# A list-scheduled order for a hash attention with a feed-forward layer: later loads on the Pool queue, more transposes by DMA

## The chip, the cores and the metric

The kernel runs on one core of one Trainium2 chip. The metric is device microseconds (us) of one execution, as the median of several runs. "Span" is the time from the first to the last instruction in the trace; the measured time of this kernel lies about 2 us above it. A run is called slow if it is over 1.5 % above the fastest run of the same kernel; ratios use fast runs alone.

## The reference

```
q, k, v: (4 batches, 8 heads, 768 rows, 64)    proj: (64, 6)
q_bits = (q @ proj > 0);  k_bits = (k @ proj > 0)          # 6 bits, one bucket per row
mask   = bucket(q)[:, None] == bucket(k)[None, :]
attn   = softmax(where(mask, q @ k.T / 8, -1e9)) @ v
x      = attn as (3072 tokens, 512)
h      = max(x @ w1, x @ w2, x @ w3)                        # 512 -> 768
out    = h @ w_out                                         # 768 -> 512, float32
```

A wrong hash bit changes whole rows, so the kernel computes the bits from both an fp16 high part and an fp16 remainder.

## The kernel before

The work comes in 16 pairs of heads (4 batches of 4 pairs). For each pair, q and k are loaded as float32 (`raw`), split into an fp16 high part and an fp16 remainder that lie side by side (`S16`, 128 columns), and transposed to operands (`T`, 128 partitions). Six hash bits per row are computed from all 128 partitions and then written over the first six remainder rows, so that a score is one product of depth 70: the 64 real columns and six columns of plus or minus a large number. Where all six bits agree, the exp's bias brings the score back to size; elsewhere it underflows to zero.

Batches 0 and 1 are transposed by TensorE (PE), batches 2 and 3 by transposing DMAs. All loads of q, k and v and all transposing DMAs go through the SP queue, in a hand-made order of steps.

```
    def load(n, b, pr, eng, heads=(0, 2)):
        h0, h1 = heads
        r_ = raw_tile(n, b, pr)
        src = {"q": q, "k": k, "v": v}[n][b, 2 * pr + h0 : 2 * pr + h1]
        eng.dma_start(r_[:, h0:h1, :], src.rearrange("h (p c) d -> p h (c d)", c=NCH))
    # ... cut ...
    def xbar(n, b, pr):
        nc.sync.dma_start_transpose(T[n, b, pr][:], S16[n, b, pr][:].rearrange("p a d -> p (a d)"))
    # ... cut ...
    def score(u):                                    # two matmuls, then the exp
        # ... cut ...
        nc.scalar.activation(AT[:], sc[:, :, 0:HQ], ActFn.Exp, bias=bias_t[:], scale=EXP_SCALE)
    # ... cut: attend (AT times v, 12 small matmuls per two units), norm, x_T ...
    def push_ffn(b, hf, xT):
        # l1: 4 matmuls of 128x384 into "ps", 18 times; l2: 6 matmuls of 128x512 into "po", 3 times
    # ... cut ...
    for b in range(1, B):
        for pr in range(NP):
            s = 33 + 7 * pr if b == 1 else 2 * (b - 1) * NUG + 4 + 11 * pr
            at(s - 8, lambda b=b, pr=pr: load_pair(b, pr, nc.sync))
            (front if b == 1 else prep)(b, pr, s)        # front: PE transposes; prep: DMA transposes
```

There are 192 score units of two matmuls each, 192 exps, and 8 blocks of the feed-forward layer (FFN; "ps" is its first layer, "po" its second). A block can start only when all four pairs of its half batch have been attended. PE takes its instructions in the order in which they were written: if the next one waits for an operand, all later ones wait too.

The softmax here doesn't subtract the row's maximum and nothing guards it: scores larger than these inputs give would overflow.

Of the kernel before, what the change touches and what calls it, by code (L numbers as in the profile page):

```python
# [8 lines left out]
FP32 = mybir.dt.float32  # L10
# [3 lines left out]


@with_exitstack
def kernel(
# [24 lines left out]
    KR = D + NBITS  # L42

# [5 lines left out]

    konst = ctx.enter_context(tc.tile_pool(name="konst", bufs=1))  # L50
    raw = ctx.enter_context(tc.tile_pool(name="raw", bufs=4))
    spl = ctx.enter_context(tc.tile_pool(name="spl", bufs=3))
    opnd = ctx.enter_context(tc.tile_pool(name="opnd", bufs=8))
    vpool = ctx.enter_context(tc.tile_pool(name="vpool", bufs=2))
    atp = ctx.enter_context(tc.tile_pool(name="atp", bufs=4))
    small = ctx.enter_context(tc.tile_pool(name="small", bufs=4))
    xp = ctx.enter_context(tc.tile_pool(name="xp", bufs=3))
    hp = ctx.enter_context(tc.tile_pool(name="hp", bufs=12))
    op = ctx.enter_context(tc.tile_pool(name="op", bufs=4))
# [5 lines left out]


    raws = {}

    def raw_tile(n, b, pr):
        if (n, b, pr) not in raws:  # L70
            raws[n, b, pr] = raw.tile([P, 2, NCH * D], FP32, tag=n + "32", name=n + "32")
        return raws[n, b, pr]

    def load(n, b, pr, eng, heads=(0, 2)):
        h0, h1 = heads
        r_ = raw_tile(n, b, pr)
        src = {"q": q, "k": k, "v": v}[n][b, 2 * pr + h0 : 2 * pr + h1]
        eng.dma_start(r_[:, h0:h1, :], src.rearrange("h (p c) d -> p h (c d)", c=NCH))
# [3 lines left out]
    load("q", 0, 0, nc.sync, (0, 1))  # L82
    load("k", 0, 0, nc.sync, (0, 1))
    load("q", 0, 0, nc.sync, (1, 2))
    load("k", 0, 0, nc.sync, (1, 2))
    load("v", 0, 0, nc.sync)
    for n in "qkv":
        load(n, 0, 1, nc.sync)

    bias_t = konst.tile([P, 1], FP32, name="bias_t")  # L90
    nc.vector.memset(bias_t[:], EXP_BIAS)
    warm = konst.tile([P, 1], FP32, name="warm")
    nc.scalar.activation(warm[:], bias_t[:], ActFn.Exp)
    iden = konst.tile([P, P], FP16, name="iden")
    make_identity(nc, iden[:])
    ones = konst.tile([P, P], FP16, name="ones")
    nc.vector.memset(ones[:], 1.0)
    vones = []
    for i in range(2):
        t = konst.tile([P, H, NCH, D + 2], FP16, name=f"vone{i}", tag=f"vone{i}")  # L100
        nc.vector.memset(t[:, :, :, D : D + 1], 1.0)
        vones.append(t)

    ph = konst.tile([D, NBITS], FP16, name="ph")
    pr32 = konst.tile([D, NBITS], FP32, name="pr32")
    PA, PB = [], []
    for i in range(2):
        for n, l in (("PA", PA), ("PB", PB)):
            l.append(konst.tile([P, 32], FP16, name=f"{n}{i}", tag=f"{n}{i}"))
            nc.vector.memset(l[i][:], 0.0)  # L110

    def make_p(i):

        if i == 0:
            nc.vector.tensor_copy(ph[:], p32[:])
            nc.vector.tensor_tensor(out=pr32[:], in0=p32[:], in1=ph[:], op=AluOp.subtract)
        for o in (0, D):
            for l, src in ((PA, ph), (PB, pr32)):
                nc.vector.tensor_scalar(out=l[i][o : o + D, NBITS * i : NBITS * (i + 1)], in0=src[:],
                                        scalar1=1024.0, scalar2=None, op0=AluOp.mult)  # L120

    w_sb = [konst.tile([P, NJ, DF], FP16, name=f"w{i}_sb") for i in range(3)]
    wout_sb = konst.tile([P, NF, DM], FP16, name="wout_sb")

    def load_w(i, half):
        w_ap = (moe_w1, moe_w2, moe_w3)[i].rearrange("(c p) f -> p c f", p=P)
        f = slice(half * DF // 2, (half + 1) * DF // 2)
        nc.gpsimd.dma_start(w_sb[i][:, :, f], w_ap[:, :, f])


    T = {}
    S16 = {}

    def operands(b, pr):
        for n in "qk":
            S16[n, b, pr] = spl.tile([P, 2 * NCH, 2 * D], FP16, tag=n + "s", name=n + "s")
            T[n, b, pr] = opnd.tile([P, 2 * NCH, P], FP16, tag=n + "T", name=n + "T")

    def split_h(n, b, pr, eng, heads=(0, 2)):
        a = slice(heads[0] * NCH, heads[1] * NCH)  # L140
        x32 = raws[n, b, pr][:].rearrange("p h (c d) -> p (h c) d", d=D)[:, a, :]
        o = S16[n, b, pr][:, a, 0:D]
        if eng is nc.scalar:
            nc.scalar.activation(o, x32, ActFn.Copy, scale=QS)
        else:
            eng.tensor_scalar(out=o, in0=x32, scalar1=QS, scalar2=None, op0=AluOp.mult)  # L146

    def split_r(n, b, pr, heads=(0, 2)):
        a = slice(heads[0] * NCH, heads[1] * NCH)
        x32 = raws[n, b, pr][:].rearrange("p h (c d) -> p (h c) d", d=D)[:, a, :]  # L150
        s = S16[n, b, pr]
        nc.vector.scalar_tensor_tensor(out=s[:, a, D : 2 * D], in0=x32, scalar=QS,  # L152
                                       in1=s[:, a, 0:D], op0=AluOp.mult, op1=AluOp.subtract)

    def xbar(n, b, pr):
        nc.sync.dma_start_transpose(T[n, b, pr][:], S16[n, b, pr][:].rearrange("p a d -> p (a d)"))

    def pe_T(n, b, pr, hh):
        ps = mm_ps.tile([P, 512], FP32, tag="mm", name="tps")
        p16 = ps[:].bitcast(FP16)  # L160
        for c in range(NCH):
            nc.tensor.transpose(p16[:, c * P : (c + 1) * P], S16[n, b, pr][:, hh * NCH + c, :], iden[:])  # L162
        return p16

    def evac_T(p16, n, b, pr, hh, eng, c0=0, c1=NCH):
        o = T[n, b, pr][:, hh * NCH + c0 : hh * NCH + c1, :].rearrange("p a t -> p (a t)")
        if eng is nc.scalar:
            nc.scalar.copy(o, p16[:, c0 * P : c1 * P])
        else:
            nc.vector.tensor_copy(o, p16[:, c0 * P : c1 * P])  # L170

    def hash_mm(sets):

        hps = mm_ps.tile([P, 512], FP32, tag="mm", name="hps")
        ws = [(i, l[i]) for l in (PA, PB) for i in range(len(sets))]
        for m, (i, w) in enumerate(ws):
            for g, (t, hh, half) in enumerate(sets[i]):
                a = hh * NCH + half * CH
                nc.tensor.matmul(hps[32 * g : 32 * (g + 1), 0:HQ], w[:], t[:, a : a + CH, :],  # L179
                                 start=m == 0, stop=m == len(ws) - 1)  # L180
        return hps

    def hash_cmp(out, hps):
        nc.vector.tensor_scalar(out=out, in0=hps[:, 0:HQ], scalar1=0.0, scalar2=0.5,  # L184
                                op0=AluOp.is_gt, op1=AluOp.subtract)

    def hash_row(dst, src):
        nc.vector.tensor_scalar(out=dst, in0=src, scalar1=2 * BIT, scalar2=None, op0=AluOp.mult)  # L188

    hbs = {}  # L190

    def hash_pair(b, pr):
        hb = small.tile([P, HQ], FP16, tag="hb", name="hb")
        hbs[b, pr] = hb
        g = [(T[n, b, pr], hh) for hh in range(2) for n in "qk"]
        hash_cmp(hb[:], hash_mm([[(t, hh, half) for t, hh in g] for half in range(2)]))
        hash_row(hb[:], hb[:])

    def hash_half(b, pr, half):
        if half == 0:  # L200
            hbs[b, pr] = small.tile([P, S], FP16, tag="hb2", name="hb2")
        g = [(T[n, b, pr], hh, half) for hh in range(2) for n in "qk"]
        hash_cmp(hbs[b, pr][:, half * HQ : (half + 1) * HQ], hash_mm([g]))

    def hash_head_rows(b, pr, hh):
        for i, n in enumerate("qk"):
            dst = T[n, b, pr][D : D + NBITS, hh * NCH : (hh + 1) * NCH, :].rearrange("p a t -> p (a t)")
            o = 32 * (2 * hh + i)
            hash_row(dst, hbs[b, pr][o : o + NBITS, :])

    def hash_rows(b, pr):
        hb = hbs.pop((b, pr))
        for g, (n, hh) in enumerate((("q", 0), ("k", 0), ("q", 1), ("k", 1))):
            for half in range(2):
                a = hh * NCH + half * CH
                o = 32 * g + NBITS * half
                nc.sync.dma_start(T[n, b, pr][D : D + NBITS, a : a + CH, :].rearrange("p a t -> p (a t)"),
                                  hb[o : o + NBITS, :])

    def hash_head(b, pr, hh):  # L220

        tq, tk = T["q", b, pr], T["k", b, pr]
        hb = small.tile([P, HQ], FP16, tag="hb", name="hb")
        hash_cmp(hb[:], hash_mm([[(tk, hh, 0), (tq, hh, 0), (tk, hh, 1), (tq, hh, 1)]]))
        for g, (t, half) in enumerate(((tk, 0), (tq, 0), (tk, 1), (tq, 1))):
            a = hh * NCH + half * CH
            hash_row(t[D : D + NBITS, a : a + CH, :].rearrange("p a t -> p (a t)"),
                     hb[32 * g : 32 * g + NBITS, :])
# [290 lines left out]
```

## Time and profile before

| | before |
|---|---|
| time, median of 3 runs | 308.07 us (307.59 to 308.14) |
| span, mean clock granted to TensorE | 306.0 us, 0.974 |
| PE busy | 276.1 us (90 %) |
| first "ps" matmul | 63.9 us |
| last exp | 281.0 us |

The profile's page: busy time by engine with its share of the span; then the span in 40 equal slices (7.65 us each), a digit being tenths of the slice; then one group of instructions with its busy time and the mean ns of one.

```profile
span 306.0 us, 7090 instructions
...
PE 276.1 (90%) x2896; PEld 176.6 (58%) x2896; DVE 212.0 (69%) x455; ACT 200.6 (66%) x265; POOL 9.3 (3%) x17
...
PE   3847888989969989999999989999999999999994
...
PEclk9969979999997999999999999999999999999998
DMA  7999940006326285915809490926002001100202
...
L269 ACT ACTIVATE AT<-sc,bias_t 128x768 f16<-128x768 f32 x192 | 169.1, 902 | 73.2 <-PE sc L265 72.7
...
```

PE is at nine tenths or more in most slices once the first 60 us are over; the exp takes 902 ns.

The table of stretches of the same kernel: the stretch, its length, busy us and instruction count of each engine, then the granted clock, the mean busy share of the 16 DMA engines and the GB/s moved. The DMA share adds up the recorded times of packets, and it exceeds 1 in places.

```profile
core 0: us, PE busy (x) PEld busy (x) DVE busy (x) ACT busy (x) POOL busy (x), PEclk, DMA share, GB/s
60.00:160.00 100.00, 93.18 (x1044) 60.23 (x1043) 77.83 (x165) 71.01 (x93) 0.00 (x0) 0.98 0.46 121
160.00:280.00 120.00, 118.94 (x1207) 74.83 (x1205) 76.39 (x161) 89.30 (x121) 0.00 (x0) 1.00 0.35 83
...
```

The tile view of the first FFN layer shows the shortest, median and longest matmul in ns and the first and last start:

```profile
...
L329 PE MATMUL ps<-xT,w_sb x576: 322/326/527, 63.9 to 297.3; 128*128 128x384 f16 x192
...
```

The view of waits (us in total, times, longest) shows that ACT waits for scores, that is, for PE, and the longest wait of PE's matmuls for an operand, 4.3 us for a split at the start:

```profile
engine line waited for: us in total, times, longest us
ACT AT L269 <- PE sc L265: 72.7, 101, 5.5
...
PE tps L162 <- DVE qs L152: 11.9, 7, 4.3
...
```

### The profile page before, as it was taken

Reading aid. Unit: us, or ns where it says so; the run is one execution under the profiler, and the core shown is the slowest. Engines: PE = TensorE matmul, PEld = TensorE weight load, DVE = VectorE, ACT = ScalarE, POOL = GpSimd, SP = SyncE. Lnnn points to the kernel's source line nnn. Section 1 sums busy time; section 2 is a strip of 40 time slices with the busy share of each in tenths; the row PEclk is TensorE's granted clock in tenths of the full one; section 3 lists DMA queues with packets and bytes.
Section 4 is the critical chain, followed back from the end, with each engine's and each line's share of the span. In section 5 each row is a group of like instructions: output and inputs, shape, how many; then the busy total and the mean of one; then the engine's idle time right before and its main releaser. Section 6 shows DMA issues by size and latency. Waiting matters only on the chain.

```text
span 306.0 us, 7090 instructions
## 1 busy us (share of the span) xinstructions
PE 276.1 (90%) x2896; PEld 176.6 (58%) x2896; DVE 212.0 (69%) x455; ACT 200.6 (66%) x265; POOL 9.3 (3%) x17
## 2 busy tenths in 40 slices
PE   3847888989969989999999989999999999999994
PEld 1444565656646656565666556656666665666551
DVE  5687996877995867969587677969664454455551
ACT  3425658968646667777778676868676787786220
POOL 1370000000000000000000000000000000000000
PEclk9969979999997999999999999999999999999998
DMA  7999940006326285915809490926002001100202
GB/s 216 372 287 264 227 131 2 3 5 185 132 56 172 45 233 130 222 39 113 249 15 230 114 246 20 237 95 136 2 1 105 2 0 54 53 1 2 103 0 104
DMA packets 46080, 35.20 MB, mean 115 GB/s; under 512 B 26656, under 2 KB 42976, under 8 KB 46048
## 3 DMA queue, kind: packets, MB, share of 16 engines
q1 hardware_dynamic: 42016, 31.61, 37.7%
q0 software_dynamic: 3952, 3.15, 6.5%
q8 instruction: 22, 0.36, 0.5%
q14 instruction: 10, 0.08, 0.1%
q10 hardware_dynamic: 80, 0.00, 0.0%
HBM read 25.17 MB, written 6.29 MB: 103 GB/s over the span
## 4 chain that ended last, share of the span: by engine, by line
PE 74%; DVE 18%; ACT 3%; issue 2%; DMA 1%; SPq 0%; DVEq 0%; ACTq 0%
PE ps L329 28%; PE sc L265 16%; PE av L285 9%; PE po L341 9%; PE hps L179 4%; PE tps L162 4%; DVE qs L152 3%; ACT AT L269 2%; DVE hb L184 2%; DVE ks L146 2%; DVE ks L152 2%; PE xps L315 2%; DVE kT L188 2%; PE svp L244 1%; DVE t L301 1%
## 5 line engine op out<-in xcount | busy, mean ns | idle before, releaser
L269 ACT ACTIVATE AT<-sc,bias_t 128x768 f16<-128x768 f32 x192 | 169.1, 902 | 73.2 <-PE sc L265 72.7
L329 PE MATMUL ps<-xT,w_sb 128*128 128x384 f16 x576 | 112.4, 327 | 1.9 <-DVE ht L336 1.7
L265 PE MATMUL sc<-qT,kT 70*128 70x384 f16 x384 | 96.4, 332 | 4.2 <-ACT AT L269 1.6
L285 PEld LDWEIGHTS <-AT 128*128 128x128 f16 x1152 | 61.3, 98 | 31.1 <-issue 6.9
L336 DVE TENSOR_TENSOR ht<-ht,ps 128x384 f16<-128x384 f16 x96 | 52.9, 552 | 34.4 <-PE ps L329 31.6
L285 PE MATMUL av<-vone,AT 128*128 128x65 f16 x1152 | 67.1, 193 | 4.4 <-DVE t L301 4.3
L329 PEld LDWEIGHTS <-w_sb 128*128 128x128 f16 x576 | 50.8, 98 | 30.9 <-issue 5.8
L265 PEld LDWEIGHTS <-kT 70*128 70x128 f16 x384 | 34.0, 100 | 23.9 <-issue 6.4
L341 PE MATMUL po<-wout_sb,ht 128*128 128x512 f16 x144 | 34.8, 379 | 0.0
L334 ACT CAST ht<-ps 128x384 f16<-128x384 f32 x48 | 22.8, 474 | 16.3 <-PE ps L329 16.1
L301 DVE TENSOR_TENSOR t<-av,mv 128x390 f32<-128x390 f32 x32 | 17.9, 560 | 10.1 <-PE av L285 10.0
L184 DVE TENSOR_SCALAR hb<-hps 128x384 f16<-128x384 f32 x28 | 15.2, 553 | 8.7 <-PE hps L179 8.6
L162 PE MATMUL tps<-iden,qs 128*128 128x128 f16 x96 | 9.7, 259 | 12.7 <-DVE qs L152 11.9
L341 PEld LDWEIGHTS <-ht 128*128 128x128 f16 x144 | 12.8, 97 | 13.1 <-issue 0.6
L347 DVE COPY osb<-po 128x512 f32<-128x512 f32 x16 | 11.0, 688 | 11.5 <-PE po L341 11.5
L305 DVE TENSOR_TENSOR xn<-t,rr 128x384 f16<-128x384 f32 x32 | 17.9, 558 | 1.1
L152 DVE SCALAR_TENSOR_TENSOR qs<-q,qs 128x768 f16<-128x768 f32 (+1 forms) x17 | 16.5, 972 | 0.1
L162 PEld LDWEIGHTS <-qs 128*128 128x128 f16 x96 | 7.4, 116 | 14.7 <-DVE qs L152 13.3
L316 DVE COPY xT<-xps 128x384 f16<-128x384 f16 x32 | 11.3, 353 | 6.2 <-PE xps L315 5.9
L152 DVE SCALAR_TENSOR_TENSOR ks<-k,ks 128x768 f16<-128x768 f32 (+1 forms) x17 | 15.3, 906 | 0.3
L179 PE MATMUL hps<-kT,PA 128*32 128x384 f16 x64 | 11.1, 343 | 1.0 <-DVE kT L170 0.9
L170 DVE COPY kT<-tps 128x768 f16<-128x768 f16 x16 | 8.6, 553 | 4.3 <-PE tps L162 4.2
(43 smaller groups left out, 172.9 us busy)
## 6 DMA issues: line engine op xcount, KB each, us to landing
v<-in_v_dram SPq DMA_DIRECT2D x16, 384.0 KB
out_dram<-osb SPq DMA_DIRECT2D x24, 256.0 KB
q<-in_q_dram SPq DMA_DIRECT2D x15, 384.0 KB
k<-in_k_dram SPq DMA_DIRECT2D x15, 384.0 KB
w_sb<-in_moe_w_dram POOLq DMA_DIRECT2D x6, 384.0 KB, 13.3
wout_sb<-in_moe_w_out_dram POOLq DMA_DIRECT2D x1, 768.0 KB, 22.0
q<-in_q_dram SPq DMA_DIRECT2D x2, 192.0 KB
k<-in_k_dram SPq DMA_DIRECT2D x2, 192.0 KB
```

The source lines that it names most:

```text
L152: nc.vector.scalar_tensor_tensor(out=s[:, a, D : 2 * D], in0=x32, scalar=QS, in1=s[:, a, 0:D], op0=AluOp.mult, op1=AluOp.subtract)
L162: nc.tensor.transpose(p16[:, c * P : (c + 1) * P], S16[n, b, pr][:, hh * NCH + c, :], iden[:])
L179: nc.tensor.matmul(hps[32 * g : 32 * (g + 1), 0:HQ], w[:], t[:, a : a + CH, :], start=m == 0, stop=m == len(ws) - 1)
L184: nc.vector.tensor_scalar(out=out, in0=hps[:, 0:HQ], scalar1=0.0, scalar2=0.5, op0=AluOp.is_gt, op1=AluOp.subtract)
L265: nc.tensor.matmul(sc[:, i, 0:HQ], kT[0:KR, hh * NCH + 2 * j + i, :], qT[0:KR, hh * NCH + hf * CH : hh * NCH + (hf + 1) * CH, :], start=Tr ...
L269: nc.scalar.activation(AT[:], sc[:, :, 0:HQ], ActFn.Exp, bias=bias_t[:], scale=EXP_SCALE)
L285: nc.tensor.matmul(av[:, o : o + D + 1], AT[:, i, c * P : (c + 1) * P], vones[b % 2][:, 2 * pr + hh, 2 * j + i, 0 : D + 1], start=first, s ...
L301: nc.vector.tensor_tensor(out=t[:, :, :, 0 : D + 1], in0=av[:, :, :, 0 : D + 1], in1=mvs[b, pr][:].unsqueeze(2).to_broadcast([P, 2, CH, D ...
L329: nc.tensor.matmul(ps[:, 0:HQ], w_sb[i][:, jc, fb * P : (fb + 1) * P], xT[:, jc, :], start=jc == 0, stop=jc == NJ - 1)
L334: nc.scalar.copy(ht[:], ps[:, 0:HQ])
L336: nc.vector.tensor_tensor(out=hts[fb][:], in0=hts[fb][:], in1=ps[:, 0:HQ], op=AluOp.max)
L341: nc.tensor.matmul(ps[:], hts[fb][:, c * P : (c + 1) * P], wout_sb[:, fb, :], start=fb == 0, stop=fb == NF - 1)
```

## The change

The intent: replace the hand-made steps by a list scheduler that, with planned durations and buffer counts, decides the order of every engine's instructions before the kernel is built; let ready FFN work fill PE where scores are not ready; keep transposes on SP from waiting behind loads (in the kernel before, SP's loads, L78, waited twice for DVE's splits to free a buffer, 17.1 us in all, by the view of SP's waits), by giving the loads of batches 1 to 3 to the Pool queue; score pair 0 one head at a time, as the kernel before already does, so that the first exp needs only one head's operands; take the exp's bias as a constant; compute the hash with T as weights and 12 columns, transpose the bits, and bring them to T through a small DRAM tile. Batch 1's operands and most of x's blocks are now transposed by DMA too: 24 operand transposes where there were 16, each 393 KB as before, and 20 of x where there were none.

The planner's DMA model is worth reading: a transfer takes its planned time, 1.8 times that if another queue is moving data, plus 2 us to land. A transposing DMA of one operand is planned at 2.1 us and a load at 1.1 us.

```diff
+class Plan:
+    LAT = {"PE": 0.22, "DVE": 0.1, "ACT": 0.1, "POOL": 0.1, "SP": 2.0}
... cut ...
+                    if t.xfer:
+                        at = max(dma.get(e, 0.0), now + dur)
+                        shared = any(x > at for r, x in dma.items() if r != e)
+                        dma[e] = at + t.xfer * (1.8 if shared else 1.0)
+                        end = dma[e] + 2.0
... cut ...
+    plan = Plan({"sc": 2, "av": 1, "mm": 3, "at": 5, "q": 4, "k": 4, "v": 4, "s": 4, "T": 8,
+                 "xn": 6, "xT": XT, "ht": HT, "osb": OSB, "bit": 2, "bt": 2, "dr": 4, "t": 2})
... cut ...
-        eng.dma_start(r_[:, h0:h1, :], src.rearrange("h (p c) d -> p h (c d)", c=NCH))
+        ENG[e].dma_start(raws[n, b, pr][:, h0:h1, :], x.rearrange("h (p c) d -> p h (c d)", c=NCH))
... cut ...
-        nc.scalar.activation(AT[:], sc[:, :, 0:HQ], ActFn.Exp, bias=bias_t[:], scale=EXP_SCALE)
+        nc.scalar.activation(AT[:], scs.pop(u)[:, :, 0:HQ], ActFn.Exp, bias=EXP_BIAS, scale=EXP_SCALE)
... cut ...
-    blocks = [(0, hf, pr) for pr, hf in ((0, 0), (0, 1), (1, 0), (1, 1), (2, 0), (3, 0), (2, 1), (3, 1))]
+    blocks = [(0, 0, ((0, 0), (1, 0))), (0, 0, ((0, 1), (1, 1)))]
... cut ...
+        by_pe = b == 0
+        if b > 0:
+            gate = {0: wload[0, 2], 1: wload[1, 0], 2: wload[1, 2], 3: wload["o"]}[pr] if b == 1 else None
+            for n in "qkv":
+                before = loads.get((n, b, pr - 1, (0, 2))) or loads.get((n, b - 1, NP - 1, (0, 2)))
+                loads[n, b, pr, (0, 2)] = add(("POOL", 0.75), U - 40, [gate, before], lambda e, n=n: load(n, b, pr, (0, 2), e),
+                                              take=(n,), xfer=1.1)
... cut ...
+                ev.append(add(("SP", 1.4), p0 + 2, rs, lambda e, n=n: xbar(n, b, pr, e), xfer=2.1, after=ev[:1],
+                              take=("T",) if n == "q" else (), give=("s",) if n == "k" else ()))
```

## The prediction

> **What bounds it now.** Between 100 and 300 us TensorE is the limit: the table of stretches has PE busy 198 of 200 us. That overstates work, so I count pitches from the timeline: score pair 0.33 us, six attends 0.183, first-layer group (ps) 0.652, second-layer group (po) 1.29, hash set of eight 0.37, six transposes 0.34, mean-v 0.36. Times counts, that stretch holds 194 us of work: 97%. The whole kernel holds about 260 us of work in a 306 us span. Nearly all of the 46 us lost lie before 100: the first ps starts at 63.9 us, ACT waits for scores in gaps up to 5.5 us (view of waits), and from 64 to 100 us DVE is busy 29.9 of 36 us with splits, hash rows and evacuations.
>
> **What the change does.**
> 1. PE: transposes of operands fall from 192 to 120 (-4 us), of x from 96 to 36 (-3.3), mean-v matmuls from 96 to 36 (-4). Hash: 256 wide matmuls become 384 of 12 columns with T as weights; at the attend pitch of 0.03 an estimated 11 us, as before; 30 bit transposes (+2). Total about 247 us.
> 2. ACT: exp loses its bias tile. It takes 0.90 us, pitch 0.79. [...] I expect 0.81-0.83, pitch 0.73: -12 us. ACT takes splits and evacuations from DVE (+20).
> 3. DVE: hash rows and half the splits and evacuations go; an estimated 165 us, 212 now.
> 4. Later loads and weights go to the Pool queue, so that SP's transposes no longer queue behind loads that wait for a buffer; bits go through DRAM. The list-scheduled order runs operands a batch ahead (all hashes by score 112 of 192) and puts FFN groups where scores are not ready.
>
> **Critical path.** PE is the limit once FFN work exists. 39 score units precede the first ps. The first score comes later (11 us against 8.8: two rounds of transposes), then ACT paces: 39 x 0.73 plus 8 us of other ACT work puts the first ps at 48 us. PE work issued by then is 32 us; the other 214.5 at 97% take 221. Span = 48 + 221 + 4.5 (last store, as now) = 274; measured time is 2 us above the span: **276 us**, 8 in 10 between 267 and 288. Of 32 us, 13 are less PE work, 19 closed gaps.
>
> **What would show it.** First ps at 44-52 us; PE busy over 97% from 60 us on; exp about 0.82 us each; last exp at 210-225 us, then some 55 us of FFN alone with PE full; DVE idle over a third of the span; hash matmuls about 0.03 us apart.
>
> **What would make it wrong.** The order is fixed in advance: if real latencies (transposing DMA, bits through DRAM, Pool-issued loads) exceed the planned ones, PE sits in order behind a hash or score whose operand is late. Pool now issues 36 loads and 36 sums; [...] a split beside Pool work at 17.6 us took 2.0 us against 0.95. Throughout, that makes 285-295. With ACT 93% busy and two score buffers, ACT could pace scores. If hash matmuls cost 0.1 us each, add 25 us.
>
> Chances: faster by over 2% 0.94, within 2% 0.04, slower 0.02.

The sum is 48 + 221 + 4.5 = 274 us of span, and 276 us with the 2 us that the measured time lies above the span. But the exp's "0.81-0.83" and the pitch of 0.73, which are in the 48 us through 39 × 0.73, stand as expectation alone; measured afterwards were 812 ns and, where one exp starts before the last has ended, 0.71 us from start to start (0.80 before; our count over the timeline). The 285 to 295 us rest on the one split: it took 2.09 us from 17.56 us on, the median of its kind 0.95.

## The result, and the profile after

The changed kernel takes **335.76 us** (331.87 to 341.98, 5 runs) against 308.14 us (307.59 to 310.41, 5 runs) of the kernel before: it is 8 % slower, and correct. The ratio is 1.0806, 95 % interval 1.0734 to 1.0879. Ratios here and below are the mean time of one kernel's fast runs over that of the other's of the same rounds, so they are not quite the ratios of the medians.

The profiled run took 338.71 us and counts as slow by the rule above; the fast runs took 331.87 to 335.76 at a clock of 0.887 to 0.889, against 0.884 here. So the profile shows what the fast runs also have, about one per cent larger.

The page after (slices are now 8.42 us):

```profile
span 336.9 us, 7243 instructions
...
PE 280.3 (83%) x2894; PEld 183.1 (54%) x2894; DVE 183.1 (54%) x402; ACT 203.3 (60%) x292; POOL 60.8 (18%) x89
...
PE   7885969987563944345999999999999999999994
...
PEclk9599675996985897575899999999999999999999
DMA  7999952599999999999169941121102000111202
...
L363 ACT ACTIVATE AT<-sc 128x768 f16<-128x768 f32 x192 | 146.9, 812 | 72.8 <-PE sc L357 71.9
...
```

The table of stretches after:

```profile
core 0: us, PE busy (x) PEld busy (x) DVE busy (x) ACT busy (x) POOL busy (x), PEclk, DMA share, GB/s
60.00:160.00 100.00, 59.76 (x599) 36.62 (x597) 52.83 (x115) 41.50 (x60) 33.92 (x48) 0.76 1.09 168
160.00:280.00 120.00, 120.00 (x1440) 80.67 (x1438) 73.06 (x161) 105.60 (x148) 2.85 (x4) 0.99 0.32 66
...
```

Against before, PE loses 33 us of busy time between 60 and 160 us, and what it does there runs at a clock of 0.76 instead of 0.98. The DMA engines show the opposite: a share of 1.09 instead of 0.46, for 168 GB/s instead of 121. After 160 us PE is full, 120.00 of 120 us. So the loss lies in one stretch. The first FFN matmul starts at 61.4 us, hardly earlier than before, and the last exp at 275.9 us:

```profile
...
L434 PE MATMUL ps<-xT,w_sb x576: 323/326/528, 61.4 to 328.3; 128*128 128x384 f16 x192
...
```

What does PE wait for? The view of the operand tile T lists how long the issue of a transposing DMA took (shortest, median and longest, ns), and for how long engines that wanted T sat idle, by what ended the wait (us, times). T<-s is a transposing DMA, T<-dr the return of the hash bits from DRAM:

```profile
L253 SPq DMA_TRANSPOSE T<-s x24: 1368/1587/16481, 52.8 to 192.6; - x24
...
its engine sat idle before it (us, times) until:
  DMA T<-s: 46.7, 8
  DMA T<-dr: 38.0, 9
...
```

The tile view adds PE and its weight loads together, which wait at the same time. The view of waits separates them; PE's own matmuls are:

```profile
...
ACT AT L363 <- PE sc L357: 71.9, 70, 11.4
...
PE hps L277 <- DMA T<-s: 23.2, 4, 10.8
...
PE sc L357 <- DMA T<-dr: 18.3, 4, 8.5
...
```

The matmuls of the hash (L277) wait 23.2 us for transposes and those of the scores (L357) 18.3 us for bits; their weight loads wait about as long at the same times. These are the new waits; before, no single operand wait of PE was over 4.3 us; now the longest are 10.8 and 8.5.

The chain of work that ended last, followed back from the end (start in us, us, what):

```profile
...
75.68 14.87 DMA T<-s
...
92.72 1.28 PE ps L434 x4
...
94.74 11.78 DMA T<-dr
...
113.85 26.76 DMA T<-s
...
148.35 8.04 DMA T<-dr
...
```

Four transfers into T make up 61 us of the chain between 75 and 157 us. A piece runs from issue to landing, so it is not all idle time: PE is busy for 23.9 of these 61 us with what still stands before the missing operand, and idle for the rest. One first-layer group stands among them: it took 1.28 us for its four matmuls, twice the 0.65 us that it takes at full clock. The planner had 2.1 us for a transposing DMA, or 3.8 us when shared, plus 2 us to land; it took 14.87 and 26.76 us. Pool's loads are slow as well: the page's list of DMA issues ends with the median us from issue to landing.

```profile
...
q<-in_q_dram POOLq DMA_DIRECT2D x12, 384.0 KB, 10.8
...
```

The timeline of the Pool queue shows when its loads were issued (start in us, us, engine, what); the first and the last load of batch 1:

```profile
...
21.43 0.71 POOL L220 DMA_DIRECT2D q<-in_q_dram  x1
...
40.86 0.72 POOL L220 DMA_DIRECT2D v<-in_v_dram  x1
...
```

The timeline of the SP queue, in the same columns, shows how long its transposes took to issue:

```profile
...
80.85 13.78 SPq L253 DMA_TRANSPOSE T<-s  x2
...
124.00 23.54 SPq L253 DMA_TRANSPOSE T<-s  x2
...
```

Twelve loads of batch 1 leave Pool between 21.4 and 41.6 us. On SP, two transposes keep the queue from 80.85 to 94.6 us, and another two from 124.00 to 147.5 us: the queue that was to be free is held up by the transposes themselves. In the timeline of SP in the kernel before, with little else moving, the issue of one took 1.45 us:

```profile
...
206.59 1.45 SPq L156 DMA_TRANSPOSE qT<-qs  x1
...
```

A transpose there with nothing beside it moved its 393 KB in 2.01 us, 196 GB/s, with the DMA share at 1.04 (211.57 to 213.58 us).

### The profile page after: what moved, and what is told of

Read it like the earlier page. It is cut to its first block, busy times and chain, and to the rows that moved or that the text cites. A ratio compares the mean times of both kernels' runs of the same rounds, so it can differ in the third digit from the quotient of the medians.

```text
span 336.9 us, 7243 instructions
## 1 busy us (share of the span) xinstructions
PE 280.3 (83%) x2894; PEld 183.1 (54%) x2894; DVE 183.1 (54%) x402; ACT 203.3 (60%) x292; POOL 60.8 (18%) x89
## 4 chain that ended last, share of the span: by engine, by line
PE 66%; DMA 23%; DVE 6%; ACT 2%; issue 1%; SPq 1%; DVEq 0%; ACTq 0%
PE ps L434 24%; PE sc L357 19%; DMA T<-s 12%; PE av L375 9%; PE po L450 9%; DMA T<-dr 8%; ACT AT L363 2%; DMA dr<-bt 2%; PE hps L277 2%; DMA k<-in_k_dram 1%; PE tps L264 1%; DVE s L243 1%; DVE ht L445 1%; PE bps L302 1%; PE xps L424 1%
## 5 line engine op out<-in xcount | busy, mean ns | idle before, releaser
L363 ACT ACTIVATE AT<-sc 128x768 f16<-128x768 f32 x192 | 146.9, 812 | 72.8 <-PE sc L357 71.9
L357 PE MATMUL sc<-T 70*128 70x384 f16 x384 | 103.5, 357 | 19.0 <-DMA T<-dr 18.3
L357 PEld LDWEIGHTS <-T 70*128 70x128 f16 x384 | 32.3, 105 | 33.7 <-DMA T<-dr 19.6
L277 PE MATMUL hps<-PAB,T 128*128 128x12 f16 x384 | 12.9, 170 | 23.2 <-DMA T<-s 23.2
L172 ACT CAST ht<-ps 128x384 f16<-128x384 f32 x27 | 12.9, 479 | 29.1 <-DVE ht L445 22.5
L392 DVE TENSOR_TENSOR t<-av,mv 128x390 f32<-128x390 f32 x32 | 17.9, 561 | 16.0 <-PE av L375 15.9
L277 PEld LDWEIGHTS <-T 128*128 128x128 f16 x384 | 12.1, 99 | 24.3 <-DMA T<-s 23.6
L172 ACT COPY osb<-po 128x512 f32<-128x512 f32 x21 | 12.3, 586 | 15.8 <-PE po L450 15.6
L174 DVE CAST ht<-ps 128x384 f16<-128x384 f32 x21 | 11.7, 556 | 15.7 <-PE ps L434 15.5
L243 DVE SCALAR_TENSOR_TENSOR s<-q,s 128x384 f16<-128x384 f32 x32 | 19.6, 628 | 1.0 <-ACT s L236 0.8
L243 DVE SCALAR_TENSOR_TENSOR s<-k,s 128x384 f16<-128x384 f32 x32 | 17.8, 577 | 0.7 <-ACT s L236 0.7
L325 POOL TENSOR_TENSOR vt<-v 128x384 f32<-128x384 f32 x12 | 12.6, 1052 | 12.7 <-DMA v<-in_v_dram 12.5
## 6 DMA issues: line engine op xcount, KB each, us to landing
q<-in_q_dram POOLq DMA_DIRECT2D x12, 384.0 KB, 10.8
```

The costliest lines, as they stand in the source:

```text
L172: nc.scalar.copy(o, i)
L243: nc.vector.scalar_tensor_tensor(out=s[:, a0:a1, D : 2 * D], in0=raw_view(n, b, pr, heads), scalar=QS, in1=s[:, a0:a1, 0:D], op0=AluOp.mul ...
L277: nc.tensor.matmul(hps[:, a * 2 * NBITS : (a + 1) * 2 * NBITS], T[b, pr][:, a, :], PAB[:], start=True, stop=True)
L325: nc.gpsimd.tensor_tensor(out=t[:], in0=v32[:, :, 0:half], in1=v32[:, :, half : 2 * half], op=AluOp.add)
L357: nc.tensor.matmul(sc[:, i, 0:HQ], t[0:KR, NA2 + hh * NCH + 2 * j + i, :], t[0:KR, hh * NCH + hf * CH : hh * NCH + (hf + 1) * CH, :], star ...
L363: nc.scalar.activation(AT[:], scs.pop(u)[:, :, 0:HQ], ActFn.Exp, bias=EXP_BIAS, scale=EXP_SCALE)
```

## The experiments

Three theories, A to C, stood at the start; D was added after the first runs, before e8.

- **A**: loads on the Pool queue and transposing DMAs on the SP queue, in flight together, slow each other, and the in-order PE stands behind the late operand.
- **B**: the new chain to an operand (split, transposing DMA, hash, bits through DRAM) is longer than planned, whoever loads.
- **C**: there are too many transposing DMAs, squeezed into one stretch.
- **D**: the weights, which are loaded at the start, delay the first bits and so the first FFN work.

All changes below are against the kernel after, unless another is named. "Before" measured 307.4 to 308.3 us in median.

| run | edit | us, median (range, runs) | ratio to before (95 %) |
|---|---|---|---|
| e1_loads_sp | later loads on SP | 294.85 (292.80–295.97, 4) | 0.9549 (0.948–0.962) |
| e2_loads_act | later loads on ACT's queue | 305.16 (302.36–312.81, 4) | 0.9891 (0.979–0.999) |
| e3b_small_loads | later loads a sixth of their size | 288.56 (284.83–290.95, 4) | 0.9346 (0.925–0.945) |
| e4b_batch1_pe | batch 1 transposed by PE | 316.26 (315.05–319.13, 4) | 1.0317 (1.021–1.042) |
| e5_batch1_pe_sp | e4b and loads on SP | 300.65 (299.98–300.87, 4) | 0.9745 (0.971–0.978) |
| e6_T5 | 5 operand tiles planned, not 8 | 307.24 (298.27–311.88, 4) | one fast run, no ratio |
| e7_T5_sp | e6 and loads on SP | 287.87 (284.95–290.08, 4) | 0.9333 (0.924–0.942) |
| e8_T5_sp_late_w | e7, weights later | 300.21 (296.35–301.72, 6) | 0.9682 (0.962–0.975) |
| e11_T5_sp_bias | e7, exp's bias from a tile | 294.86 (292.67–297.88, 4) | 0.9558 (0.949–0.962) |
| e12_fifo | e8, matmul banks planned in turn | 300.02 (298.68–300.77, 4) | 0.9758 (0.970–0.982) |
| e13_fifo_dve | e12, longer hash bits planned | 301.51 (300.57–302.05, 4) | 0.9795 (0.974–0.985) |
| e14_batch1_pe_sp_T5 | e5 with 5 operand tiles | 289.64 (285.50–291.97, 6) | 0.9408 (0.937–0.945) |
| e15_pool_512 | Pool loads cut into 512-byte rows | 344.09 (321.53–352.23, 4) | one fast run, no ratio |
| e16_pool_paced | Pool loads no earlier than ACT's place | 329.17 (315.50–332.88, 4) | one fast run, no ratio |

### Later loads on another queue

```diff
-        ENG[e].dma_start(raws[n, b, pr][:, h0:h1, :], ...)
+        nc.sync.dma_start(raws[n, b, pr][:, h0:h1, :], ...)                             # e1_loads_sp
+        (nc.scalar if b else nc.sync).dma_start(raws[n, b, pr][:, h0:h1, :], ...)        # e2_loads_act
```

The plan is untouched: the same loads are written at the same places, so every other engine keeps its order. Only the queue differs.

> Edit: the loads of batches 1 to 3 are issued on the SP queue at the same place of the planned order; all engines else keep their orders. Theory A (loads on the Pool queue and transposing DMAs on the SP queue are served at the same time[...] and both crawl: 256-byte transpose packets at 75 to 200 ns against 20 alone): loads and transposes now follow each other in one queue, so the waits of PE for T after 64 us fall from some 70 us to under 20, and the time is 280 to 300 us. Theory B (the chain transpose, hash, bits out, bits in is too long for the planned order, whoever loads): 325 to 340 us. Theory C (24 + 20 transposes and 36 loads are more than the DMA engines can carry in that stretch): 320 to 340 us, as the bytes stay the same.

> Edit: the loads of batches 1 to 3 are issued on the ACT queue [...], not on Pool; still a queue beside SP. If A holds because the queues are two: still slow, 315 to 340 us. If A holds because Pool's queue is the one[...]: 280 to 300 us. Theories B and C: 325 to 345 us. ACT itself pays about 36 x 0.4 us for issuing, mostly hidden.

The page says that Pool's queue is "software_dynamic" (q0) and SP's "hardware_dynamic" (q1). On the packet times of theory A: of the 19,477 packets of 256 bytes that start between 75 and 160 us in the kernel after, the median took 18 ns, 569 took 75 to 200 ns and 1,127 longer (our count).

With SP, 294.85 us; with ACT, 305.16 us. One word takes 41 us away from the changed kernel. The stretches from 60 to 160 us of e1 and then of e2, in the columns of the tables above:

```profile
...
60.00:160.00 100.00, 89.67 (x1094) 59.14 (x1092) 79.58 (x181) 74.39 (x108) 23.13 (x30) 0.93 1.02 226
...
60.00:160.00 100.00, 82.21 (x969) 53.25 (x966) 75.65 (x167) 67.28 (x97) 22.40 (x30) 0.88 1.10 224
...
```

In e1 the same number of transposes and the same bytes are moved, at 226 instead of 168 GB/s, with a smaller DMA share (1.02 for 1.09). Its waits for T fall to a fifth (15.9 us for 84.7):

```profile
...
  DMA T<-dr: 10.7, 6
...
  DMA T<-s: 5.2, 4
...
```

and the two transposes that are left in e1's chain take 5.77 and 5.30 us, about what the plan's rule gives for a shared one (2.1 × 1.8 + 2 = 5.8):

```profile
...
127.69 5.77 DMA T<-s
...
147.79 5.30 DMA T<-s
...
```

B falls: the chain to an operand is the same. A holds so far, with a limit: loads on ACT's queue are also on another queue than the transposes, and cost only 10 us more than on SP (305.16 us lies between the two ranges that had been expected). So "two queues" alone is not what costs 41 us; it is Pool's queue, or the moment at which Pool issues (see e16 below).

### Later loads almost taken away

```diff
+        if b > 0:
+            raws[n, b, pr] = raws[n, 0, pr]
-        ENG[e].dma_start(raws[n, b, pr][:, h0:h1, :], x.rearrange("h (p c) d -> p h (c d)", c=NCH))
+        y = x.rearrange("h (p c) d -> p h (c d)", c=NCH)
+        w = NCH * D if b == 0 else D
+        ENG[e].dma_start(raws[n, b, pr][:, h0:h1, 0:w], y[:, :, 0:w])
```

The later loads move a sixth of their columns, into batch 0's tiles, so the result is wrong (relative error 0.81). They stay on Pool, at their places.

> Edit: the changed kernel with the later loads still on Pool's queue, each moving a sixth of its bytes into batch 0's buffers (wrong result on purpose; same orders, queue and waits). After the first runs (loads on SP 294.9 us, on ACT 305.2) theory A, two queues at once slow each other, expects nearly nothing left to collide: 275 to 288 us. Theory C, too many transposes in one stretch, expects 290 to 300 (loads gone, but the transposes still queue). Theory B, latency of the chain whoever loads, is already weakened and expects above 325.

It takes 288.56 us, just above A's range and below C's. Its stretch from 60 to 160 us:

```profile
...
60.00:160.00 100.00, 93.38 (x1191) 62.83 (x1190) 88.76 (x192) 81.25 (x118) 37.93 (x52) 0.98 0.77 139
...
```

and two pieces of its chain at the start, in the columns of the chain above (dr<-bt takes the hash bits to DRAM):

```profile
...
22.33 5.21 DMA dr<-bt
27.62 5.05 DMA T<-dr
...
```

All 24 operand transposes and 20 of x are still there, with the same DRAM round trips and the same Pool instructions. So 47 us of the changed kernel (335.8 − 288.6) go with the later loads' bytes. This also disposes of a worry of the prediction, that Pool's work slows DVE's splits (2.09 us against 0.95 above): e3b keeps Pool's sums and its 36 issues of 0.7 us, so they cannot be the cause of these 47 us.

The 47 us (50 between the two profiled spans) can be split by the pages of the two kernels, which run the same 2,894 matmuls. PE is busy 280.3 us in the kernel after and 264.3 in e3b; it is idle 336.9 − 280.3 = 56.6 and 286.8 − 264.3 = 22.5 us. So 34 us are waits, and 16 us are the same matmuls at a lower clock (by the trace's clock record, PE is busy at half clock for 56.1 us in the kernel after and 16.4 in e3b; our count). The trace of the kernel after shows waits and lower clock together: PE is idle for 3.98 us from 86.6 us on, waiting for the transpose of 14.87 us, and the clock record stands at half from 91.24 to 94.65 us, where the group in the chain took 1.28 us, twice its usual time. So it is with all six stretches of over 3 us in which PE does nothing (3.57 to 10.85 us): the record goes to half during them or at most 1.04 us after their end. It also does so three times without one (from 9.32, 46.87 and 77.59 us), so a wait of that length is not its only cause (our count). In this trace a long wait is paid twice.

### Fewer transposing DMAs

```diff
-        by_pe = b == 0
+        by_pe = b <= 1
-                    ev.append(add(both(0.5, 0.72), p0 + 3, [t], ...
+                    ev.append(add(both(0.5, 0.72), p0 + 3 if b == 0 else URGENT, [t], ...
-                                  give=("mm",) + (("s",) if (n, hh) == ("k", 1) else ())))
+                                  give=("mm",) + (("s",) if (n, hh) == ("k", 1) and b == 0 else ())))
-        hm = add(("PE", 0.67), p0 + 4, ev + [mp], ..., take=("mm",))
+        hm = add(("PE", 0.67), p0 + 4, ev + [mp], ..., take=("mm",), give=("s",) if b == 1 and by_pe else ())
```

Batch 1's operands go back to PE: 16 transposing DMAs instead of 24. With the first line alone (e4_batch1_pe) the kernel deadlocks when it is built; the other lines mend that. e5_batch1_pe_sp adds e1's edit, and e14_batch1_pe_sp_T5 the one of the next section.

> Edit: the changed kernel, batch 1 transposed by PE (8 of 24 transposing DMAs of T go; evacuations made urgent so that it builds; order planned anew), loads still on Pool. Theory A: the stretch to about 100 us mends, that of batches 2 and 3 does not: 305 to 325 us. Theory C (too many transposes): 290 to 305 us.

> Edit: loads on SP (the 294.9 us version) and batch 1 transposed by PE. The loads-on-SP run keeps the DMA engines over 100% busy from 56 to 150 us. Theory C, DMA demand is what is left: 8 transposing DMAs of about 2 us fewer against 16 x 0.34 = 5.4 us more PE work: 284 to 291 us. If PE and DVE in that stretch are what is left (DVE 90 to 98% busy), the four evacuations more per pair make it 296 to 304 us.

> Edit: the same with 5 operand tiles ahead and not 8 (287.9 us with batch 1 on DMA). Theory C: 280 to 287 us. If PE and DVE work is what is left: 290 to 297 us.

With loads on Pool, a third fewer transposes give 19.5 us (316.26 for 335.76). With loads on SP they give no gain: 300.65 against 294.85 of e1, and 289.64 against 287.87 of e7. So the number of transposes matters only where they are slow, as far as these runs can say: each of the three was planned anew, so the whole order changed with the transposes. C as a theory of the whole loss falls, by e1 above all. In e14's table of stretches PE is 97 us of 100 busy at full clock, but part of that work is now the 96 transposes that came back to it.

Transposing all batches on PE with Pool loads would have shown whether ordinary transfers suffer from Pool's loads as the transposes do. No form of it that we tried could be built, so this is left open.

### Fewer operands ahead

```diff
-    plan = Plan({"sc": 2, "av": 1, "mm": 3, "at": 5, "q": 4, "k": 4, "v": 4, "s": 4, "T": 8,
+    plan = Plan({"sc": 2, "av": 1, "mm": 3, "at": 5, "q": 4, "k": 4, "v": 4, "s": 4, "T": 5,
```

The planner believes in five operand tiles instead of eight, so it starts later pairs later and spreads the DMA work. e7_T5_sp adds e1's edit.

> Edit: the planner may hold 5 operand tiles ahead and not 8, so splits, transposes and with them the loads of batches 2 and 3 spread over the kernel (last hash at score 156 and not 112); loads still on Pool's queue. Theory A with bursts as the trouble: fewer loads meet each transpose, 300 to 320 us. If each transpose meets one burst of loads anyway, the same 330 to 340 us.

> Edit: as before it (5 operand tiles ahead), and the later loads on the SP queue. Theory C, the demand on the DMA engines compressed into 56 to 150 us (share over 1.0 there in the run with loads on SP): spreading it gives 280 to 290 us against 294.9. If what is left is not DMA demand: 293 to 300 us.

With Pool loads it takes 307.24 us, with a wide spread (298.27 to 311.88). That is 28.5 us less than the kernel after on the same queue, and the view of T adds up to 40.9 us of waits in place of 84.7: spreading the work eases the collision, as A expected of bursts. With SP loads, 287.87 us, the fastest correct kernel: 48 us under the changed kernel and 6.7 % under the kernel before. Its stretch:

```profile
...
60.00:160.00 100.00, 93.50 (x1142) 61.97 (x1140) 81.95 (x184) 83.75 (x118) 22.06 (x30) 0.97 0.88 204
...
```

The DMA share is 0.88 instead of e1's 1.02, and the time 7 us shorter (287.87 for 294.85). That agrees with the part of C that says that the DMA work was squeezed too tightly; the order was planned anew here too, so it is not shown that the share is the cause.

### The weights at the start

In e7 the first FFN work still starts at 55.5 us (tile view of "ps"), where 44 to 52 had been predicted. In e3b's chain above, the hash bits of pair 1 take 5.21 us to DRAM and 5.05 us back, while the seven weight loads are in flight; later in the kernel after (at 45.7 us), the way back took 2.17 us. So the weights were held back until the exp of unit 11:

```diff
+        if u == GATE:
+            nc.scalar.copy(w_sb[0][:, 0, 0:1], AT[:, 0, 0:1])
+    GATE = 11
+                if u == GATE:
+                    for w in wload.values():
+                        w.deps.append(x)
```

> Edit: loads on SP and 5 operand tiles ahead, as in the run that took 287.9 us; in addition the weight loads on Pool wait (by a one-element write into w) for the exp of unit 11, so that they start near 29 us and not at 14. The hash bits of pair 1 then cross DRAM without the weights: 4 to 6 us for both ways in place of 10.6 (21.1 to 31.7 us). Theory D, the weights at the start are the same collision once more: first ps at 49 to 52 us (55.5 before), 281 to 285 us. If the two ways take 10 us whatever runs beside them: no gain, or a loss of a few us as the weights come late.

It takes 300.21 us, 12 us more: the expectation failed. The profile is of a slow run (301.67 us; fast ones 296.35 to 299.12). The early stretches of e7:

```profile
...
8.00:24.00 16.00, 13.62 (x192) 11.26 (x189) 14.62 (x32) 12.29 (x18) 8.89 (x11) 0.79 1.17 283
24.00:54.00 30.00, 23.81 (x318) 17.38 (x319) 16.83 (x41) 21.90 (x30) 1.91 (x3) 0.89 0.69 149
...
```

and of e8:

```profile
...
8.00:24.00 16.00, 14.55 (x242) 12.28 (x238) 15.43 (x36) 14.13 (x22) 3.69 (x4) 0.89 0.55 191
24.00:54.00 30.00, 23.60 (x268) 16.13 (x269) 11.63 (x30) 20.31 (x29) 7.38 (x10) 0.77 0.92 177
...
```

The start is relieved, as D says: the DMA share falls from 1.17 to 0.55 between 8 and 24 us. But the first "ps" comes at 53.7 us, only 1.8 us earlier, and what was not moved then is moved later: 0.92 for 0.69 from 24 to 54 us. Pair 1's bits go out in 1.6 us (19.10 to 20.67) where e7 needed 5.6 (21.10 to 26.68), but the collision only moves on to pair 3, whose bits leave at 31.01 us, are fetched at 36.42 and land at 41.41, with the weights in flight. Further on, the chain of e8 holds loads of batches 1 (the first line) and 2 that e7's chain does not have:

```profile
...
76.94 5.01 DMA v<-in_v_dram
...
90.35 5.15 DMA q<-in_q_dram
...
```

We read this as: the early DMA time is not idle time to be saved; it is capacity that the later stretch lacks. It is not shown, because the plan puts the loads of batch 1 behind the weights, so that they moved too (the first leaves at 36.73 us, in e7 at 27.95). Two more versions asked whether the planner's optimism about PSUM banks (it takes any free bank, the kernel takes them in turn) or about DVE's hash bits (planned 0.85 us, measured 0.29 + 0.80 + 0.30) keeps e8 slow:

```diff
+                        if "mm" in t.take and banks and min(banks.values()) <= nbank - 3:
+                            continue                                                    # e12_fifo
-        hb = add(("DVE", 0.85), p0 + 5, [hm], ...
+        hb = add(("DVE", 1.3), p0 + 5, [hm], ...                                         # e13_fifo_dve, also 0.75 -> 1.1
```

> Edit: the late-weights version; the planner lets a matmul bank be taken only when the one three before it is free (the three banks are used in turn, which the plan did not know). If hidden waits for banks cost time: 2 to 5 us less than the late-weights version. If not: the same within 2 us.

> Edit: as the one before it, and the planner is told 1.3 us for the hash bits on DVE in place of 0.85 (measured: 0.30 + 0.80 + 0.29). A better plan for the stretch 56 to 112 us, in which DVE is 90 to 98% busy: 0 to 4 us less; a plan this sensitive may also get worse by as much.

Neither helps (300.02 and 301.51 us against 300.21; by fast runs alone, 1.7 and 3.2 us more than e8's median of 298.36).

### The bias of the exp

```diff
+    bias_t = konst.tile([P, 1], FP32, name="bias_t")
+    nc.vector.memset(bias_t[:], EXP_BIAS)
-        nc.scalar.activation(AT[:], scs.pop(u)[:, :, 0:HQ], ActFn.Exp, bias=EXP_BIAS, scale=EXP_SCALE)
+        nc.scalar.activation(AT[:], scs.pop(u)[:, :, 0:HQ], ActFn.Exp, bias=bias_t[:], scale=EXP_SCALE)
```

> Edit: the 287.9 us version with the exp's bias read from a tile again. Exp 0.90 us each, 0.79 apart, 192 x 0.06 to 0.07 = 12 to 13 us more of ACT. As ACT is over 90% busy from 100 to 220 us here, I expect 5 to 12 us more (293 to 300 us); if PE alone is the limit there, under 3 us more.

With the bias from a tile, e7 takes 294.86 us, 7 us more, and the exp 910 ns instead of 812. This part of the change is a real gain. Neighbouring exps overlap (in the kernel after, 85 of them start before the one before has ended, 0.10 us before in the median; our count), so the busy time of all 192 falls by 16 us (162.1 to 146.1, from the two pages), of which 7 us are seen in the time; that ACT paces only a part of the kernel would explain the rest, but was not tested.

### Why Pool's queue and not ACT's

The packet records of the trace, counted by size and queue (this is our own count, not a view of the profile; times in ns; 256-byte packets are those of the transposes and, in all but "before", 2,160 of hash bits; 1536-byte packets on SP include the loads of batch 0; Pool's queue also sends 576 packets of 1536 bytes):

```
                 256 bytes, SP                  loads of q, k, v                            all packets / 16 engines
before           24576, median 18, mean 26.1    1536 bytes, SP,   median  65, mean  74.3   137 us
after            46704, median 18, mean 33.1    4608 bytes, Pool, median 195, mean 278.7   207 us
e1_loads_sp      46704, median 18, mean 24.8    1536 bytes, SP,   median  65, mean  77.1   174 us
e2_loads_act     46704, median 18, mean 24.5    1536 bytes, ACT,  median  65, mean  93.1   182 us
e7_T5_sp         46704, median 18, mean 24.6    1536 bytes, SP,   median  65, mean  76.1   173 us
```

The loads are the same instruction on the same data, but Pool's queue sends them as packets of 4608 bytes. The transposes' packets keep their median of 18 ns, but 1,182 of them take over 200 ns in the kernel after, against 324 in e1 and 181 in e2; their sum rises by (33.1 − 24.8) × 46,704 / 16 = 24 us per engine, most of the 33 us by which the total differs from e1. That a transpose packet waits behind a large one is the author's guess at it; no run shows in which order packets are served. In the stretch from 60 to 160 us fewer bytes move, 168 GB/s against 226, at a higher share of recorded packet time. Whether that is a real loss of throughput or packets that are recorded while they wait, the trace does not tell; so the mechanism is not shown. And large packets on Pool's queue do not do it by themselves: in e3b they are of 4096 bytes, but only 576 of them, and the 256-byte packets there have a mean of 24.9 ns, as in e1.

Two runs tried to isolate the packet. e15_pool_512 cut each Pool load into three with rows of 512 bytes; e16_pool_paced let ACT write one element of the raw tile before each Pool load, so that Pool could not issue it earlier than ACT had in e2.

```diff
+        y = x.rearrange("h (p c) d -> p h (c d)", c=NCH)
+        w = NCH * D if b == 0 else 2 * D
+        for o in range(0, NCH * D, w):
+            ENG[e].dma_start(raws[n, b, pr][:, h0:h1, o : o + w], y[:, :, o : o + w])     # e15_pool_512
+        if b > 0:
+            nc.scalar.copy(raws[n, b, pr][:, 0, 0:1], warm[:])                            # e16_pool_paced
```

> Edit: the changed kernel, each later load on Pool cut into three of 512 bytes a row (108 in place of 36; same bytes, same queue). The packets of Pool's loads are 4608 bytes in the trace, three rows of 1536; a load on SP or ACT goes in packets of 1536. If the size of the packet that stands before each 256-byte transpose packet is what makes Pool (335 us) worse than ACT (305 us), smaller packets give 305 to 320 us. If the rows are put together to 4608 again, or the size is not it: 330 to 345 us.

> Edit: the changed kernel; ahead of each later load ACT writes one element of its tile, so that the load stays on Pool's queue but starts no earlier than ACT has reached its place in the order, as in the run with loads on ACT (12 loads between 21 and 42 us become 3). If Pool is worse than ACT because it runs ahead and sends its loads in bursts: 300 to 312 us. If because of its queue and packets: 325 to 340 us.

e15 did not make the test: the queue put the 512-byte rows together to packets of 4096 bytes (our count), and the time was as bad (344.09 us, 321.53 to 352.23). e16 takes 329.17 us, inside the range expected if the queue and its packets are the cause; its one fast run, 315.50 us, lies between the fast runs of the kernel after (331.87 to 335.76) and of e2 (302.36 to 306.49). Its stretch and its waits for T (profile of a run of 332.26 us, slow by the rule):

```profile
...
60.00:160.00 100.00, 61.43 (x605) 37.02 (x604) 56.17 (x117) 42.84 (x82) 31.78 (x46) 0.71 1.16 166
...
  DMA T<-s: 15.9, 6
  DMA T<-dr: 15.6, 6
...
```

The waits for T fall from 84.7 to 31.5 us, but PE is no busier in the stretch (61.43 us for 59.76). Loads that leave later also land later: the chain now holds three loads of q of 7 to 9 us. The edit exchanges one late operand for another, so it does not separate the moment from the queue. That the early moment is a part of the loss is not shown by it either: e15, without pacing, has a run of 321.53 us. In e16 Pool's packets are of 4608 bytes too, and their mean is 329.7 ns; whether it is their size is not settled. These runs spread by up to 10 %, more than those with loads on SP (1 to 2 %), so medians a few per cent apart say little here.

## Why the prediction was wrong

**The step that failed** is item 4, "Later loads and weights go to the Pool queue, so that SP's transposes no longer queue behind loads that wait for a buffer", which was counted as a gain, and with it "PE is the limit once FFN work exists … the other 214.5 at 97% take 221". The runs show the reverse: moving the loads to Pool costs 41 us (335.76 against 294.85 of e1), and from 60 to 160 us PE was busy 59.76 us, not 97. Transposes that shared the queue with the loads took 5 to 6 us in e1's chain; freed from it they took 14.87 and 26.76. The prediction did name this risk under "What would make it wrong" (late operands from "transposing DMA, bits through DRAM, Pool-issued loads" before an in-order PE) but gave it no size (its 285 to 295 us are for DVE's splits beside Pool's work), and gave 0.02 to a slower kernel.

Two terms were missing from its sum. Long waits come with a lower clock of PE, and 16 of the 50 us of span between the kernel after and e3b are that. And the DMA work was never added up by stretch: the packets of the kernel before make 137 us per engine in the whole span, a share of 0.46 from 60 to 160 us; 44 transposing DMAs instead of 16, next to loads issued as early as buffers allow, made 1.09 of it (e1 has 1.02 and takes 294.85 us, so this sum alone is not the loss).

**Right, as predicted.** About 13 us less PE work: where PE is not slowed it is busy 264.3 us (e3b) and 265.6 (e1), 276.1 before. The exp at "0.81-0.83": measured 812 ns, 90 ns less. e11, which puts the bias tile back into e7, measured 910 ns, 98 more. PE full after the trouble: 120.00 of 120 us from 160. "Some 55 us of FFN alone" after the last exp: from 275.9 us to the end of PE's work near 333, 57 us. DVE idle over a third: 46 % (in a longer span; 35 % in e3b). Hash matmuls about 0.03 us apart: 24 of them start within 0.58 us (0.025 apart).

**Wrong, besides the failed step.** First "ps" at "44-52 us": 61.4 us in the kernel after, and still 55.5 and 56.5 us in e7 and e3b, which have no such trouble. The prediction had the first score at 11 us; it started at 14.1. And it let ACT alone pace the way from there, while e3b's chain waits 10.3 us for the hash bits of pair 1 to pass through DRAM, which was not in the sum. Last exp at "210-225": 275.9 us, but 225.8 in e3b and 222.2 in e7. DVE at 165 us: 183.1. The prediction also counts the weights among what goes to Pool's queue; they were there before.

**What is left of 276.** With the later loads nearly gone the kernel takes 288.6 us, 12.6 us above the prediction. Of these, 8.5 us are the first "ps" (56.5 against 48). The rest, 4 us, we did not trace. So the gain of the schedule itself is real: e7 beats the kernel before by 20 us (287.87 against 307.44), about three fifths of the predicted 32 us, once the loads are on SP and five operand tiles are planned.

**What stays open**: how the loss of the Pool queue divides between the early moment of its loads, its packets and whatever else Pool does to move them; whether ordinary transfers of another queue would suffer as transposes do (Pool's own loads are slow: e15's chain holds some of 12 to 16 us); and why the DRAM round trip beside the weights costs 10 us (e8 shows that it shortens without them, and returns for the pair that meets them).

## What to carry to other kernels

Moving transfers to an idle queue is not free: here transposes in the chain took 14.87 and 26.76 us beside Pool's loads, and 5.77 and 5.30 us with the loads on their own queue. So add up the work of the DMA engines by stretch, and look at what else is in flight before counting the move as a gain; test it with the one-word edit of the queue. A static order makes one late operand stop everything behind it (8.5 us for one score), and on PE the long waits were paid a second time in clock (16 of 50 us here), so plan DMA latencies from a trace in which the same transfers run together. Early DMA time that looks wasted may be capacity that a later stretch needs.
